# First block of a three-stage float32 kernel on unsplit weights, with a shorter float64 decoding and re-strided regrouping transfers

## The chip, the cores and the metric

The kernel runs on 1 core of one Trainium2 chip. The metric is device time in microseconds (us) of one execution, as the median of several. TensorE (PE) multiplies, VectorE (DVE) and ScalarE (ACT) do elementwise work, SyncE (SP) issues all DMAs from one queue in order.

## The reference, cut to what matters

```python
# 1. gated linear attention, 4 batches x 8 heads x 768 steps x 48 dims (float32)
new_re = ar * S_re - ai * S_im ; new_im = ar * S_im + ai * S_re
S_re, S_im = new_re + outer(k_t, v_t), new_im
y_t = q_t @ S_re
# x = y as 3072 tokens x 384
# 2. first MLP
h = x @ w_in                      # 384 -> 2048
g = h * clip(h + 3, 0, 6) / 6
x2 = g @ w_out                    # 2048 -> 384
# 3. second MLP
out = ((x2 @ w1) * (x2 @ w2) @ w3) @ w_out2
```

The weights of stages 2 and 3 arrive as float64, because they are drawn times a float64 scalar; everything else is float32.

## The kernel before, in words

**Attention.** The 24 units of 128 tokens ("chunks", six per batch) are taken in 12 groups of two. `group` (L502) computes a group's decays, phases, scaled k and q on ACT and DVE with 768-wide operations, ends with the products Kc and cs (L568, L576), and regroups them head by head with `regroup` (L570): six DMAs of 16 partitions each into KT and six into QT. `chunk` (L602) then runs a chunk on PE: transposes of Kc (L618), scores (L627) whose masked copies P are made on DVE (L630), P times v and state times q (L639, L644), and the update of the state (L653), which DVE scales by a factor that travels in two extra columns of QT (L577, L656). All these matmuls are float32: the trace shows two instructions, here called passes, for each of them.

**Splitting.** The MLP matmuls run in a faster reduced type (fp32r in the profile). So that nothing is lost, every operand is split into a high part (ACT copy) and a low part (DVE subtraction), and `mm3` (L664) multiplies three times: high x high, high x low, low x high.

**Decoding.** `load64` (L669) brings in a piece of float64 weights, `to32` (L676) turns it into float32 by integer operations on the two 32-bit words of each number: two DVE operations, three ACT operations (a scaled copy, Abs, Sign) and a DVE product. `decode` (L704) follows with `split`. The first MLP has 8 + 8 pieces of 128x768, the second 12 such pieces and 16 of 128x512.

**Blocks.** The first MLP goes in blocks of 2, 2, 4, 4, 4, 4, 4 chunks. Blocks 0 and 1 (256 tokens each) run together, block 1 seven steps behind, while the weights are still being decoded; from block 2 on a block has 512 tokens, so its matmuls are 512 columns wide. `s1` (L765) makes one of the 16 slices of h: 9 matmuls, the gate (ACT Relu, DVE product, L789 to L790), and the split of its result into gh and gl. `s2` (L796) adds the slice into three accumulators m with 9 matmuls. The copy of a group's attention output into the block's input goes by six DMAs (L586), followed by a split into xh and xl (L599, L600).

**Order.** Nothing is written out by hand. Every operation is given to `Plan.add` with an estimated duration, due times follow from pins on the MLP's matmuls, and `Plan.run` (L104) emits the instructions of each engine in the order of a simulated run. Each engine then works its list strictly in order. An edit of a duration, a dependence or a buffer can thus move instructions everywhere.

```python
def to32(raw, words, n, dst, ov):
    DVE(..., tensor_scalar(words(0) >> 29 ^ 0x40000000), [], [raw])
    DVE(..., scalar_tensor_tensor(words(1) << 3 ^ words(0)), [], [raw])
    ACT(..., words(1) <- Copy(words(1) as f32, scale=16400.0) as int), [raw], [raw])
    ACT(..., words(0) <- Abs(words(0)), [raw], [raw])
    ACT(..., words(1) <- Sign(words(1)), [raw], [raw])
    DVE(..., ov <- words(0) * words(1), [raw], [dst])
```

Of the kernel before, what the change touches and what calls it, by code (L numbers as in the profile page):

```python
# [243 lines left out]
def c_tt(n):  # L244
    return n / 960.0 + 0.07


def c_ts(n):
    return n / 1920.0 + 0.07

# [148 lines left out]
def main_kernel(tc, q, k, v, a_re, a_im, w_in, w_out, w1, w2, w3, w_out2, consts, qT, kT, arT, aiT, vT, wiT, woT, w1T, w2T, w3T, wo2T, out, blocks=(2, 2, 4, 4, 4, 4, 4)):  # L399
# [22 lines left out]
    with tc.tile_pool(name="keep", bufs=1) as kp:  # L422
      c5_ = kp.tile([128, 2, 128], F32, name="c2")
      flag = kp.tile([1, 1], I32, name="flag")
      with ctx:
# [76 lines left out]
        def group(gi):  # L502
# [42 lines left out]
            cs = nb("cs", [128, 2, KD, TG + GT])  # L545
            ACT(cA, lambda: A(cs()[:, 0, :, :TG], th(), AF.Abs), [th], [cs])
# [9 lines left out]

            def sincos():
                A(cs()[:, 1, :, :TG], th(), AF.Sin, scale=TWOPI)
                A(cs()[:, 0, :, :TG], cs()[:, 0, :, :TG], AF.Sin, scale=-TWOPI, bias=PI / 2)
# [3 lines left out]
            KT, QT = nb("KT", [96, H, TG]), nb("QT", [96, H, TG + GT])  # L563

            def prod(o, f):
                for a in range(2):
                    TT(o()[:, a, :, :TG], cs()[:, a, :, :TG], f(), ALU.mult)
# [9 lines left out]
            DVE(0.17, lambda: dve.tensor_copy(out=cs()[:, :, :, TG:], in_=G()[:, :, 127:TG:128].unsqueeze(1).to_broadcast([128, 2, KD, GT])), [G], [cs])  # L577
            regroup(QT, cs, TG + GT)
            ys = nb("ys", [128, 4, C, 128])
            for c in range(C):  # L580
                chunk(b * CPB + c0 + c, c, Kc, KT, QT, ys)

            xf = nb("xf", [128, KD, TG])
            for i in range(KD):
                for j in range(2):
                    DMA(lambda e, i=i, j=j: e.dma_start(out=xf()[64 * j:64 * j + 64, i, :], in_=ys()[64 * j + 16 * i:64 * j + 16 * i + 16].rearrange("e p c t -> e p (c t)")),  # L586
                        [ys], [xf], 180000, part=True)
            u = b * CPB + c0
            j = next(j for j, (a, n) in enumerate(blk) if a <= u < a + n)
            if j not in xbuf:  # L590
# [11 lines left out]
        def chunk(u, c_, Kc, KT, QT, ys):  # L602
# [8 lines left out]
            if not last:  # L611
                Ks = nb("Ks", [128, H, 96])
                for a in range(2):
# [6 lines left out]
                    ACT(c_act(384, True), lambda a=a, pk=pk: A(Ks()[:, :, 48 * a:48 * a + 48].rearrange("p h (t d) -> p h t d", t=KD), pk().rearrange("p (t d h) -> p h t d", t=KD, h=H), AF.Copy), [pk], [Ks], part=True)  # L620
# [27 lines left out]
            if not last:  # L648
# [7 lines left out]
                mb = lambda: QT()[:, :, TG + c_:TG + c_ + 1].to_broadcast([96, H, D])  # L656
                o_ = An.ap[:, :, 0:D]
                if first:
                    DVE(c_tt(384), lambda: TT(o_, pu(), mb(), ALU.mult), [pu, QT], [An])
                else:  # L660
                    DVE(c_tt(384), lambda: TT(o_, pu(), Ap.ap[:, :, 0:D], ALU.add), [pu, Ap], [An])
                    DVE(c_tt(384), lambda: TT(o_, o_, mb(), ALU.mult), [QT], [An])
# [13 lines left out]
        def to32(raw, words, n, dst, ov):  # L676


            DVE(c_ts(n), lambda: dve.tensor_scalar(out=words(0), in0=words(0), scalar1=29, scalar2=0x40000000, op0=ALU.logical_shift_right, op1=ALU.bitwise_xor), [], [raw])
            DVE(c_tt(n), lambda: dve.scalar_tensor_tensor(out=words(0), in0=words(1), scalar=3, in1=words(0), op0=ALU.logical_shift_left, op1=ALU.bitwise_xor), [], [raw])  # L680

            ACT(c_act(n), lambda: A(words(1), words(1).bitcast(F32), AF.Copy, scale=16400.0), [raw], [raw])
            ACT(c_act(n), lambda: A(words(0).bitcast(F32), words(0).bitcast(F32), AF.Abs), [raw], [raw])
# [20 lines left out]
        def decode(src, i, after=()):  # L704
            loads[0] += 1
            if loads[0] > EARLY:
                after = list(after) + [ready0]
# [406 lines left out]
```

## Time and profile before

| what | value |
|---|---|
| median of 3 runs | 988.65 us (987.92 to 990.36) |
| the profiled execution's own time | 994.61 us |
| its span, first to last instruction | 992.4 us |
| PE busy | 905.8 us, 91% |
| DVE busy | 602.4 us, 61% |
| ACT busy | 558.7 us, 56% |
| mean granted TensorE clock | 0.983 of full speed |
| DMA queue q1 | 101.94 MB, 40.6% of 16 engines |

PE is busy nine tenths of the span, but the share differs by stage: the page's 40 slices show PE at 0, 4, 4, 7 tenths in the first four (25 us each) and at 9 in nearly all that follow, while DVE stands at 9 and ACT at 9 to 7 in the second to the sixth. A busy PE is not a PE at its full pace: its clock has two levels, 1.2 and 2.4 GHz, and at the lower one the same instructions keep it busy twice as long.

### The profile page before, as it was taken

How to read it: one execution, taken by the hardware profiler on the slowest of the kernel's cores; microseconds unless marked ns; L12 is line 12 of the kernel's file. 1: busy time of each engine (PE TensorE's matmuls, PEld its weight loads, DVE VectorE, ACT ScalarE, POOL GpSimd, SP SyncE). 2: the span in 40 equal slices, each digit the busy share in tenths (PEclk: the TensorE clock that was granted, in tenths of full speed). 3: DMA queues.
4: the chain of work that ended last, by engine and by line, in shares of the span. 5: the costliest groups of instructions: out<-in, count | busy, mean ns of one | idle time of the engine just before them, and what ended most of it. 6: DMA issues, size and time to landing. Idle time of an engine off the chain costs nothing.

```text
span 992.4 us, 13406 instructions
## 1 busy us (share of the span) xinstructions
PE 905.8 (91%) x5178; PEld 781.8 (79%) x5178; DVE 602.4 (61%) x931; ACT 558.7 (56%) x895; POOL 0.2 (0%) x4
## 2 busy tenths in 40 slices
PE   0447999889999999899999999999999999999996
PEld 0437989768887888788788878789888888888886
DVE  6899999888498839784854546995232323222221
ACT  7999998778387648565742455894121212121211
POOL 0000000000000000000000000000000000000000
PEclk9999999879999999799999999999999999999999
DMA  6896147772786086507632544732010100000000
GB/s 248 170 378 125 30 96 148 147 125 59 108 207 165 27 150 149 165 22 132 152 99 42 116 152 159 296 118 86 1 51 13 50 14 24 20 10 24 5 28 35
DMA packets 56375, 102.87 MB, mean 104 GB/s; under 512 B 6768, under 2 KB 34544, under 8 KB 56304
## 3 DMA queue, kind: packets, MB, share of 16 engines
q1 hardware_dynamic: 56304, 101.94, 40.6%
q8 instruction: 42, 0.69, 0.3%
q14 instruction: 29, 0.24, 0.1%
HBM read 64.62 MB, written 13.63 MB: 79 GB/s over the span
## 4 chain that ended last, share of the span: by engine, by line
PE 69%; ACT 15%; DVE 7%; DMA 4%; SPq 2%; issue 2%; ACTq 0%; DVEq 0%
PE x L666 12%; PE x L667 12%; PE x L665 12%; PE m L665 5%; ACT W L483 5%; PE m L666 4%; PE m L667 4%; ACT u L483 3%; PE x L627 3%; PE m L996 3%; PE m L994 3%; PE m L995 3%; ACT L1032 2%; PE x L639 1%; PE x L653 1%
## 5 line engine op out<-in xcount | busy, mean ns | idle before, releaser
L483 ACT ACTIVATE r<-x 128x512 f32<-128x512 f32 (+1 forms) x160 | 88.2, 551 | 155.2 <-PE x L667 129.4
L486 DVE TENSOR_TENSOR r<-r,x 128x512 f32<-128x512 f32 x48 | 33.0, 688 | 179.4 <-PE x L667 179.4
L665 PE MATMUL m<-gh,W 128*128 128x512 f32 (+1 forms) x336 | 126.8, 377 | 1.4 <-ACT gh L483 1.3
L666 PE MATMUL m<-gl,W 128*128 128x512 f32 (+1 forms) x336 | 124.2, 370 | 2.3 <-DVE gl L486 2.2
L483 ACT ACTIVATE W<-W 128x768 f32<-128x768 int32 (+6 forms) x153 | 121.0, 834 | 8.3 <-DVE W L680 7.1
L667 PE MATMUL m<-gh,W 128*128 128x512 f32 (+1 forms) x336 | 123.3, 367 | 0.1
L665 PE MATMUL x<-xh,W 128*128 128x512 f32 (+1 forms) x288 | 113.4, 394 | 3.8 <-ACT xh L483 3.8
L486 DVE TENSOR_TENSOR gl<-r,gh 128x512 fp32r<-128x512 f32 (+1 forms) x112 | 68.3, 611 | 78.6 <-ACT gh L483 78.3
L666 PE MATMUL x<-xl,W 128*128 128x512 f32 (+1 forms) x288 | 111.6, 387 | 3.2 <-DVE xl L486 3.2
L667 PE MATMUL x<-xh,W 128*128 128x512 f32 (+1 forms) x288 | 110.6, 384 | 0.0
L483 ACT ACTIVATE gh<-r 128x512 fp32r<-128x512 f32 (+1 forms) x112 | 63.7, 569 | 78.1 <-PE m L667 73.6
L666 PE MATMUL x<-W 128*128 128x512 f32 (+1 forms) x228 | 84.2, 369 | 0.0
L667 PE MATMUL x<-W 128*128 128x512 f32 (+1 forms) x228 | 84.2, 369 | 0.0
L665 PE MATMUL x<-W 128*128 128x512 f32 (+1 forms) x228 | 83.9, 368 | 0.0
L790 DVE SCALAR_TENSOR_TENSOR r<-r,x 128x512 f32<-128x512 f32 (+1 forms) x112 | 67.9, 606 | 25.4 <-ACT r L483 24.5
L666 PEld LDWEIGHTS m<-gl,W 128*128 128x128 f32 x336 | 64.3, 192 | 15.1 <-DVE gl L486 4.9
L665 PEld LDWEIGHTS m<-gh,W 128*128 128x128 f32 x336 | 64.3, 191 | 14.6 <-issue 2.4
L667 PEld LDWEIGHTS m<-gh,W 128*128 128x128 f32 x336 | 64.2, 191 | 11.2 <-DVE W L486 0.3
L665 PEld LDWEIGHTS x<-xh,W 128*128 128x128 f32 x288 | 56.2, 195 | 15.4 <-ACT xh L483 4.8
L666 PEld LDWEIGHTS x<-xl,W 128*128 128x128 f32 x288 | 56.3, 195 | 14.7 <-DVE xl L486 4.4
L667 PEld LDWEIGHTS x<-xh,W 128*128 128x128 f32 x288 | 56.2, 195 | 11.2
L627 PE MATMUL x<-QT,KT 96*128 96x128 f32 x384 | 54.2, 300 | 8.8 <-issue 3.3
(194 smaller groups left out, 1810.7 us busy)
## 6 DMA issues: line engine op xcount, KB each, us to landing
QT<-cs SPq DMA_DIRECT2D x72, 129.0 KB, 6.5
KT<-Kc SPq DMA_DIRECT2D x72, 128.0 KB, 5.3
W<-in_w3T_dram SPq DMA_DIRECT2D x16, 512.0 KB, 4.8
v<-in_vT_dram SPq DMA_DIRECT2D x24, 256.0 KB, 5.0
W<-in_wiT_dram SPq DMA_DIRECT2D x8, 768.0 KB, 11.7
W<-in_woT_dram SPq DMA_DIRECT2D x8, 768.0 KB, 13.1
ar<-in_arT_dram SPq DMA_DIRECT2D x12, 384.0 KB, 3.6
ai<-in_aiT_dram SPq DMA_DIRECT2D x12, 384.0 KB, 3.2
```

The costliest lines, as they stand in the source:

```text
L483: act.activation(out=o, in_=i, func=f, scale=scale, bias=bias, **kw)
L486: dve.tensor_tensor(out=o, in0=i0, in1=i1, op=op)
L627: pe.matmul(p_()[:, i, :], KT()[:, 4 * g + i, tok], QT()[:, 4 * g + i, tok])
L639: pe.matmul(py()[64 * j:64 * j + 64, p, :], vb.ap[:, h, :], Pm[h // 4]()[:, h % 4, :], start=True, stop=first, tile_position=(0, 64 * j), ...
L665: pe.matmul(o, wh, xh, start=start, stop=False, **kw)
L666: pe.matmul(o, wh, xl, start=False, stop=False, **kw)
L667: pe.matmul(o, wl, xh, start=False, stop=stop, **kw)
L790: DVE(c_tt(n), lambda: dve.scalar_tensor_tensor(out=r()[:, :n], in0=r()[:, :n], scalar=6.0, in1=h()[:, :n], op0=ALU.min, op1=ALU.mult), [h ...
L994: pe.matmul(o, gh()[:, a], Wb()[:, 0, i % 2], start=(i == 0), stop=False)
L995: pe.matmul(o, gh()[:, a], Wb()[:, 1, i % 2], start=False, stop=False)
L996: pe.matmul(o, gl()[:, a], Wb()[:, 0, i % 2], start=False, stop=(i == KI - 1))
L1032: P.run(lambda t_: act.preload_act_table_set(t_), window=48, hold=2.24)
```

## The change

- **Block 0 unsplit** (`NATIVE = 1`). The input of block 0 is written by the transfers straight into the tile xh and read as float32; there is no split of it. Its `s1` and `s2` take one float32 matmul where three fp32r ones stood, on the decoded but unsplit weights. The gate writes its tile (gh or gl, by turns) and is not split.
- **Splits follow.** `decode` no longer ends with `split`; the 16 splits of the first MLP's weights are now asked for by block 1.
- **Decoding.** `to32` has one ACT operation (a copy scaled by 2^-112) and a last DVE operation that puts sign and magnitude together; Abs and Sign are gone.
- **Regrouping.** A head's 48 rows are now ordered d*3+t where they were t*16+d, so each regrouping DMA goes to 16 partitions with a step of 3 where it went to 16 neighbours. The state's factor gets a tile of its own, mt, filled by six small DMAs per group. The planner is told smaller sizes for these transfers (800*w where it was 1408*w, 100000 where it was 180000).
- **Paced loads.** A load of first-MLP weights from the sixth on waits until the piece five before it has been taken up by DVE (`AHEAD`).

```diff
-                        DMA(lambda e, a=a, t=t: e.dma_start(out=dst()[48 * a + 16 * t:48 * a + 16 * t + 16], in_=src()[:, a, t, :]),
-                            [src], [dst], 1408 * w, part=True)
+                        DMA(lambda e, a=a, t=t: e.dma_start(out=dst()[48 * a + t:48 * a + 48:KD], in_=src()[:, a, t, :]),
+                            [src], [dst], 800 * w, part=True)
...
+            DVE(0.17, lambda: dve.tensor_copy(out=ge(), in_=G()[:, :, 127:TG:128]), [G], [ge])
+            for a in range(2):
+                for t in range(KD):
+                    DMA(lambda e, a=a, t=t: e.dma_start(out=mt()[48 * a + t:48 * a + 48:KD], in_=ge()[:, t, :]), [ge], [mt], 60000, part=True)
...
-            DVE(0.17, lambda: dve.tensor_copy(out=cs()[:, :, :, TG:], in_=G()[:, :, 127:TG:128]...), [G], [cs])
...
+            if j < NATIVE:
+                xf = SB("xh", [128, KD, NMAX], 1, F32R)
+                xbuf[j] = (xf, xf, xf, xf)
...
+            if j < NATIVE:
+                return
...
+            ACT(c_act(n), lambda: A(words(1).bitcast(F32), words(1).bitcast(F32), AF.Copy, scale=2.0 ** -112), [raw], [hi_])
+            DVE(c_ts(n), lambda: dve.tensor_scalar(out=words(0), in0=words(0), scalar1=29, ..., op0=ALU.logical_shift_right), [raw], [lo_])
+            DVE(c_tt(n), lambda: dve.scalar_tensor_tensor(out=words(0), in0=words(1), scalar=3, in1=words(0), op0=ALU.logical_shift_left, op1=ALU.bitwise_or), [hi_], [lo_])
+            DVE(c_tt(n), lambda: dve.scalar_tensor_tensor(out=ov().bitcast(I32), in0=words(1), scalar=-0x80000000, in1=words(0), op0=ALU.bitwise_and, op1=ALU.bitwise_or), [lo_], [dst])
+            return lo_
...
+        EARLY, AHEAD = 4, 5
+        taken_up = []
         def decode(src, i, after=()):
+            n_ = len(taken_up)
+            after = list(after) + ([ready0] if n_ >= EARLY else []) + ([taken_up[n_ - AHEAD]] if n_ >= AHEAD else [])
...
-            to32(raw, words, 768, raw, f)
-            return split(raw, f), shape
+            taken_up.append(to32(raw, words, 768, raw, f))
+            return raw, shape
...
+            if j == NATIVE and f % 2 == 0:
+                for w_ in (wi, wo):
+                    raw, shape = w_[f // 2]
+                    w_[f // 2] = split(raw, packed(raw, 768)), shape
...
+                    if whole:
+                        wf = packed(w, 768)().rearrange("p (a b) -> p a b", a=shape[0])
+                        pe.matmul(h()[:, :n], wf[:, kk, o:o + 128], xh()[:, kk, :n].bitcast(F32), start=kk == 0, stop=kk == KD - 1)
...
+            if whole:
+                gh = SB(("gh", "gl")[f % 2], ...)
+                ACT(..., lambda: A(gf(), h()[:, :n], AF.Relu, bias=3.0), [h], [gh], boost=MB)
+                DVE(..., scalar_tensor_tensor(out=gf(), in0=gf(), scalar=6.0, in1=h()[:, :n], op0=ALU.min, op1=ALU.mult), [h], [gh], boost=MB)
+                return gh, gh
```

In `s2` the same replacement stands with gh read as float32. New line numbers: the decoding's DVE operations are L696, L697 and L698, block 0's matmuls L806 and L837, its gate L815, the attention's transposes, scores, P times v, state times q and update L634, L643, L655, L660 and L669, `mm3` L681 to L683.

On PE, before, where block 0's first matmuls come (v and Ks are a chunk's values and keys, c the identity, W weights, xh and xl the split input):

```order
L653 MATMUL x<-v_71,Ks 96x48 x8
L618 MATMUL x<-c_58,Kc 128x128 x6
L665 MATMUL x<-xh,W 128x256
L666 MATMUL x<-xl,W 128x256
L667 MATMUL x<-xh,W 128x256
```

The same place now, from the last attention matmul of chunk 1 on (m are the accumulators of block 0):

```order
L660 MATMUL x<-QT,A_73 64x128 x2
L806 MATMUL x<-xh,W 128x256 x9
L634 MATMUL x<-c_58,Kc 128x128 x6
L837 MATMUL m_481<-gh,W 128x256
L837 MATMUL m_483<-gh,W 128x256
L837 MATMUL m_485<-gh,W 128x256
L669 MATMUL x<-v_71,Ks 96x48 x8
```

Three slices of h now stand ahead of chunk 2's transposes and update, which stood ahead of block 0.

Further on in PE's new list, where chunk 2's scores and its P times v stand between block 0's matmuls:

```order
L643 MATMUL x<-QT,KT 128x128 x8
L806 MATMUL x<-xh,W 128x256 x3
L837 MATMUL m_481<-gh,W 128x256
L837 MATMUL m_483<-gh,W 128x256
L837 MATMUL m_485<-gh,W 128x256
L655 MATMUL x<-P_574,v_71 64x128 x2
L660 MATMUL x<-QT,A_74 64x128 x2
```

All of it is float32; the first fp32r matmul of the whole list (L681, block 1) now stands behind 78 of block 0's 96 matmuls.

On DVE, before, from the low part of block 0's input to the first low part of a gate's result (r is the gate's tile, s a tile of group 2):

```order
L486 TENSOR_TENSOR xl<-xf,xh 128x3x256
L486 TENSOR_TENSOR W<-W 128x768 x3
L680 SCALAR_TENSOR_TENSOR W<-W 128x768
L790 SCALAR_TENSOR_TENSOR r<-r,x 128x256
L486 TENSOR_TENSOR W<-W 128x768
L486 TENSOR_TENSOR s_333<-s_333,u 128x768
L486 TENSOR_TENSOR gl<-r,gh 128x256
```

The place of the first gates now:

```order
L490 TENSOR_TENSOR Kc<-cs,k 128x768 x2
L815 SCALAR_TENSOR_TENSOR gh<-gh,x 128x256
L490 TENSOR_TENSOR cs<-cs,q 128x768 x2
L815 SCALAR_TENSOR_TENSOR gl<-gl,x 128x256
L697 SCALAR_TENSOR_TENSOR W<-W 128x768
```

The gates now come between the products of group 1, ahead of most of the decoding, and nothing follows a gate before PE may use it.

## Rows read from the trace of the kernel before

**Rows 1.** Busy time by stage: us, PE, PEld, DVE, ACT, POOL (instructions), PEclk, DMA share, GB/s.
```profile
0.00:81.90 81.90, 27.90 (x152) 23.74 (x152) 68.88 (x104) 73.03 (x97) 0.20 (x4) 1.00 0.84 263
...
125.00:183.00 58.00, 53.79 (x480) 51.70 (x478) 56.02 (x101) 51.18 (x95) 0.00 (x0) 1.00 0.68 127
...
206.00:420.00 214.00, 208.20 (x1193) 172.51 (x1193) 161.20 (x245) 143.14 (x224) 0.00 (x0) 0.96 0.58 128
420.00:700.00 280.00, 274.20 (x1513) 229.54 (x1512) 178.74 (x271) 164.63 (x268) 0.00 (x0) 1.00 0.45 122
```

**Rows 2.** Timeline: start us, us, engine, line, operation [idle before <- releaser].
```profile
59.22 0.68 DVE L486 TENSOR_TENSOR P<-x,c 128x512 f32<-128x512 f32 x1
...
63.91 8.86 SPq L586 DMA_DIRECT2D xf<-ys  x6
...
81.02 0.86 ACT L483 ACTIVATE xh<-xf 128x768 fp32r<-128x768 f32 x1
...
81.93 0.58 PE L665 MATMUL x<-xh,W 128*128 128x256 f32 x1 [1.63 <-ACT xh L483]
...
205.89 0.77 PE L665 MATMUL x<-xh,W 128*128 128x512 f32 x1
```

**Rows 3.** Groups by line and shape: busy us, mean ns of one, idle before it.
```profile
L680 DVE SCALAR_TENSOR_TENSOR W<-W 128x768 int32<-128x768 int32 x28 | 26.6, 952 | 0.0
...
L483 ACT ACTIVATE W<-W 128x768 f32<-128x768 int32 x28 | 26.0, 927 | 0.0
L483 ACT ACTIVATE W<-W 128x768 f32<-128x768 f32 x28 | 25.8, 926 | 0.0
...
L486 DVE TENSOR_TENSOR gl<-r,gh 128x256 fp32r<-128x256 f32 x32 | 13.3, 418 | 0.5 <-ACT gh L483 0.2
L483 ACT ACTIVATE gh<-r 128x256 fp32r<-128x256 f32 x32 | 13.3, 416 | 0.3 <-PE m L667 0.3
...
L483 ACT ACTIVATE xh<-xf 128x768 fp32r<-128x768 f32 x11 | 9.3, 845 | 6.4 <-DMA xf<-ys 4.5 <-PE x L667 1.9
```

**Rows 4.** Pieces of the chain that ended last: start us, us, what.
```profile
164.40 1.79 PE x L627 x16
...
233.03 0.81 PE x L618 x6
...
463.20 1.32 PE x L653 x16
464.51 1.02 PE x L639 x16
```

**Rows 5.** Timeline of PE in the early stage, columns as in rows 2.
```profile
46.39 3.75 PE L627 MATMUL x<-QT,KT 96*128 96x128 f32 x16 [3.33 <-issue]
...
58.49 0.70 PE L639 MATMUL x<-P,v 128*64 128x128 f32 x4 [0.45 <-DVE P L486]
...
61.53 0.64 PE L644 MATMUL x<-QT,A 96*64 96x128 f32 x4
```

**Rows 6.** Timeline of PE, fp32r matmuls of 256 columns, two stretches.
```profile
84.59 0.41 PE L667 MATMUL x<-xh,W 128*128 128x256 f32 x1
...
85.87 0.41 PE L667 MATMUL x<-xh,W 128*128 128x256 f32 x1
...
87.90 0.28 PE L665 MATMUL x<-xh,W 128*128 128x256 f32 x1
...
88.49 0.28 PE L667 MATMUL x<-xh,W 128*128 128x256 f32 x1
```

**Rows 7.** PE by stretch: us, PE busy (instructions), PEclk, DMA share, GB/s.
```profile
183.40:186.70 3.30, 3.30 (x17) 0.50 0.24 57
186.80:190.10 3.30, 3.30 (x20) 0.50 0.26 74
190.20:195.70 5.50, 5.50 (x72) 1.00 0.63 212
```

**Rows 8.** DMA issues by line: KB each, median us to landing.
```profile
KT<-Kc SPq DMA_DIRECT2D x72, 128.0 KB, 5.3
```

More of the change, by code (lines that the diff above doesn't have):

```diff
@@ L544, in group @@
                 A_prev["ce"] = ce
-            cs = nb("cs", [128, 2, KD, TG + GT])
-            ACT(cA, lambda: A(cs()[:, 0, :, :TG], th(), AF.Abs), [th], [cs])
+            cs = nb("cs", [128, 2, KD, TG])
+            ACT(cA, lambda: A(cs()[:, 0], th(), AF.Abs), [th], [cs])
+            mt = nb("mt", [96, H, GT], 2)
+            ge = nb("ge", [128, KD, GT], 2)
             y, sq = nb("u"), nb("u")
@@ L699, in pieces @@
             return src[i].rearrange("p (a b) -> p a b", a=a), (a, 768 // a)
-        EARLY = 4
-        loads = [0]
+        EARLY, AHEAD = 4, 5
+        taken_up = []
         def decode(src, i, after=()):
-            loads[0] += 1
-            if loads[0] > EARLY:
-                after = list(after) + [ready0]
+            n_ = len(taken_up)
+            after = list(after) + ([ready0] if n_ >= EARLY else []) + ([taken_up[n_ - AHEAD]] if n_ >= AHEAD else [])
             src, shape = pieces(src, i)
@@ L798, in s2 @@
             w, shape = wo[f // 2]
-            wh, wl = lambda: part(w, 0, shape), lambda: part(w, 1, shape)
             gh, gl = g
+            whole = j < NATIVE
             def mm():
+                kw = {"skip_group_check": True} if j < 2 else {}
                 for m in range(KD):
                     a = slice(m * 128, m * 128 + 128)
-                    mm3(acc[m]()[:, at:at + n], wh()[:, f % 2, a], wl()[:, f % 2, a], gh()[:, :n], gl()[:, :n], f == 0 and at == 0, f == KF - 1, **({"skip_group_check": True} if j < 2 else {}))
+                    if whole:
+                        wf = packed(w, 768)().rearrange("p (a b) -> p a b", a=shape[0])
+                        pe.matmul(acc[m]()[:, at:at + n], wf[:, f % 2, a], gh()[:, :n].bitcast(F32), start=f == 0 and at == 0, stop=f == KF - 1, **kw)
+                    else:
+                        wh, wl = part(w, 0, shape), part(w, 1, shape)
+                        mm3(acc[m]()[:, at:at + n], wh[:, f % 2, a], wl[:, f % 2, a], gh()[:, :n], gl()[:, :n], f == 0 and at == 0, f == KF - 1, **kw)
             for x in acc:
                 x.part = True
-            PE(9 * c_mm(n), mm, [w, gh, gl] + ([opened] if at else []), acc + [own] + ([] if at or f else [opened]), pin=pins["2", j, f])
+            PE(3 * c_m4(n) if whole else 9 * c_mm(n), mm, [w, gh, gl] + ([opened] if at else []), acc + [own] + ([] if at or f else [opened]), pin=pins["2", j, f])
         gens = [group(g) for g in range(NG)]
@@ L896, in later @@
             if tags is None:
-                return decode(src, g, after)
+                raw, shape = decode(src, g, after)
+                return split(raw, packed(raw, 768)), shape
             src, shape = pieces(src, g)
```

61 lines of the change are left out of this document (33 added, 28 removed).

## The prediction

> **What bounds the kernel now.** I read the stages first [rows 1]. After 206 us PE is busy for 208.2 of 214 us and 274.2 of 280 us: there the time is PE's work, and whatever ACT or DVE is spared moves the end only through the 11.6 us in which PE still waits. Up to 81.9 us it is the other way: PE is busy 27.9 us, ACT 73.0 and DVE 68.9 of 81.9. From 125 to 183 us both kinds are nearly full (PE 53.8, DVE 56.0 of 58 us). So the change can earn something only before about 206 us, where block 2 starts its 512-wide matmuls [rows 2]. I use that start as the mark: what it gains, the end gains, less the work that is pushed behind it.
>
> The timeline shows how block 0 gets started [rows 2]: the last mask of chunk 1 at 59.2, six transfers of its output issued over 8.9 us from 63.9 on, the ACT split only at 81.0, the first matmul at 81.9. PE has nothing but scraps of attention until then.
>
> **The change, part by part.**
>
> *Decoding.* Two ACT operations of 926 and 927 ns go per 128x768 piece [rows 3]; the last DVE operation keeps its length if it costs what the like integer operation costs, 952 ns. For 16 pieces this frees 16 x 1.85 = 29.7 us of ACT before block 2. ACT's copies of gh, 16 x 0.416 = 6.7 us, and of xh, 0.85 us, go too; DVE loses only 16 x 0.418 = 6.7 us of gl and about 0.95 us of xl. DVE was as full as ACT, so ACT's 37 us are mostly cover: they don't shorten the stage by themselves, DVE's 8 us might.
>
> *Start of block 0.* By the order, DVE has, ahead of the last mask of chunk 1, one shift (0.55 us) and three operations of group 1 (0.95 us each) fewer: some 3.1 us, so transfers start at 63.9 - 3.1 = 60.8. Before, they took 8.9 us to issue behind eleven weight loads; now loads are paced and I take 3.5 us for the issues and 3.3 us for landing, like the shorter of these transfers elsewhere: 60.8 + 6.8 = **67.6 us** for the first matmul, against 81.9. The bounds are 65 (DVE waits a little less for ACT) and 73 (issue as slow as before).
>
> *Block 0's matmuls.* Float32 scores run 16 passes of 128 columns in 1.79 us [rows 4] when the clock is at 2.4 GHz, so a pass of 256 columns costs 0.224 us; at 1.2 GHz 3.75 us [rows 5], 0.47 us, or twice the 0.213 us of an fp32r matmul at that level [rows 6], 0.43. I take 0.45. Block 0 has 96 matmuls, 192 passes: 43.0 us at the upper level, where 288 fp32r matmuls at 0.118 us [rows 6] cost 34.0. That is +9.0 us of PE work, beside work only as long as PE would idle anyway.
>
> *The clock* is the open question. An fp32r stretch brought it up: 0.213 us per matmul until 85.9, 0.118 from 87.9 on [rows 6]. An unbroken float32 stretch did not: from 183.4 to 186.7 PE was busy all the time with scores, at a granted 0.50, and stayed there until nine fp32r matmuls and state updates had run; from 190.2 it had 1.00 [rows 7]. So I expect block 0's first matmuls to run at 1.2 GHz, and take the dense P times v of chunk 2, two narrow passes side by side, as what brings the clock up. The trace has no such stretch inside dense work: the only one at 1.2 GHz, 58.5 to 62.2 [rows 5], has idle time on both sides. Hence this is the widest bound. The Trainium skill's page "TensorE: Matmul & The Clock Gate", section "What's actually happening", says that the default state is throttled and activity releases it, with no exception for float32. By that the clock would rise with block 0's first matmuls; the stretch at 183.4 us speaks against it, and the sum below does not use it (rival 2 does).
>
> *The sum up to the mark,* by PE's list. At 1.2 GHz from 67.6: 60 passes of block 0, 27.0; transposes 2 x 0.81 = 1.6, update 2 x 1.32 = 2.6 [rows 4], scores 3.75, P times v and state times q 3.7 [rows 5]; 38.7 in all, to 106.3. Then at 2.4 GHz: 96 passes 21.5, scores 1.8, P times v 2.0, transposes 0.8, update 1.3: 27.4, to 133.7. Then the mixed list up to the mark: 261 fp32r matmuls 30.8; 36 passes of block 0, 8.1; four groups of scores 7.2; 112 narrow passes at 1.02 / 16 = 0.064, 7.2; transposes 2.4; updates 2.6: 58.3, to 192.0. In the like stretch before, 125 to 183 us, PE was idle 4.2 of 58; I add 4. The mark comes at **196**, 9.9 us earlier than 205.9.
>
> *What is pushed behind the mark.* By the order, 16 state-update matmuls (2 x 1.32), six transposes (0.8) and 27 fp32r matmuls (27 x 0.118 = 3.2) stood ahead of it and now follow: +6.6 us.
>
> *After the mark.* ACT is relieved of 12 x 1.85 and, at about 0.67 us for 512 wide, of 16 x 1.34, in all 43.7 us. PE's waits there are 11.6 us, and a clock of 0.96 over 214 us means 17 us at the lower level, or 8.6 us lost [rows 1]. I take 4 us of these 20 as recovered, bounds 0 and 15.
>
> *Small parts.* The ge copies replace the old copies of the factor one for one: nothing. The mt transfers put 72 more issues of about 0.6 us on SP, 3.5 us a group; a group has some 33 us of SP time before 420 us: cover, unless they delay the issue of a later load. The stepped regrouping can take time off KT's 5.3 us [rows 8]; PE waits for it once early, 3.3 us at 46.4 [rows 5], but DVE's list, not the scores, sets the last mask, so the sum takes nothing. If transfers to stepped partitions were slower, the same wait would grow and the mark would slip by as much.
>
> Sum: -9.9 + 6.6 - 4 = -7.3 us. The profiled execution took 994.6 us, some 6 us more than the median; I apply the difference to the median: 988.65 - 7.3 = **981.3 us**.
>
> **The rivals.**
>
> 1. *The clock stays down through block 0 (slower).* Place: the 156 passes of block 0 ahead of the first fp32r matmul. At 1.2 GHz all the way: 70.2 us, with twice the attention's 11.8 us (23.6), from 67.6 to 161.4; then 58.3 and about 3 us until the clock is up: mark at 222.7. That is +16.8 + 6.6 - 4 = +19.4: **1008 us**. For it: the float32 stretch at 183.4 [rows 7]. Against: narrow passes side by side were never tried dense. It decides from here: every microsecond longer at the lower level after 106 costs half a microsecond, so the 7.3 us are gone if the clock is not up by about 121 us, the end of chunk 3's P times v.
>
> 2. *The clock rises at once (much faster).* As at 81.9, some 5.7 us after the first matmul, at 73.3: 33 us of work at the lower level become 16.5, the mark comes at 179.5, and the sum is -26.4 + 6.6 - 4 = -24: **965 us**. DVE could follow: it loses little work, but it is full, so not much below. Against: rows 7.
>
> 3. *No change.* The clock comes up only with chunk 3, or falls again while DVE's in-order list makes PE wait for gates; or the transfers stay slow and block 0 starts at 73. The mark then comes at 201 to 206 and its gain is eaten by the 6.6 us: **988 us**. That the transfers' new step does nothing at all belongs here and costs my sum nothing, since no term rests on it.
>
> **How the numbers follow.** Forecast 0.42, rival 1 0.27, rival 2 0.18, rival 3 0.13. About 0.3% (3 us) is what a measurement of this kernel can tell from no change. The forecast's own spread (mark 190 to 200, recovery 0 to 15) is 972 to 987, nearly all faster; rival 3 lies mostly within 0.3%. Faster: 0.40 + 0.18 = 0.58; same 0.14; slower 0.28. The range for 8 in 10 reaches from 961, a little past rival 2, to 1004, into rival 1 with a somewhat earlier start. The likeliest case alone spans 972 to 987.
>
> **What would show it.** The first block-0 matmul at 65 to 70 us; passes of 256 columns some 0.43 to 0.47 us apart at first and 0.22 after chunk 2's P times v, near 106; ACT well below DVE between 50 and 175 us; the first 512-wide matmul at 190 to 200. If passes are still 0.43 apart at 125, rival 1 has it; if they are 0.22 apart at 75, rival 2. If the mark comes early and the time doesn't fall, the step on the work behind the mark is wrong, and PE's waits after it must have grown.

## The result and the profile after

The change takes 957.49 us in the median of 4 runs (954.36 to 963.3), against 988.92 us of the kernel before in the same session: ratio 0.9688, 95% interval 0.9634 to 0.9742, 31 us faster. The prediction said 981.3 us, 961 to 1004: the sign was right, the size was not, and the time lies 3.5 us below the range. The profiled execution is the slowest of the four, 963.3 us with a span of 961.1 us, and the one before was slow for its kernel too (994.6 us), so I compare spans: 992.4 before, 961.1 after, 31.3 us less.

The engines' busy time on the page of the change (PE had 905.8 us before):

```profile
PE 898.6 (93%) x5082; PEld 772.0 (80%) x5082; DVE 592.7 (62%) x914; ACT 495.1 (52%) x790; POOL 0.2 (0%) x4
```

The stages of the change, columns as in [rows 1]:

```profile
0.00:62.80 62.80, 21.11 (x124) 18.57 (x124) 51.90 (x81) 54.20 (x72) 0.20 (x4) 0.97 0.69 238
62.80:125.00 62.20, 59.26 (x371) 52.59 (x372) 58.54 (x87) 42.84 (x69) 0.00 (x0) 0.92 0.51 141
125.00:183.00 58.00, 52.23 (x434) 48.56 (x433) 48.48 (x84) 39.25 (x71) 0.00 (x0) 0.94 0.51 142
185.00:400.00 215.00, 213.18 (x1276) 175.99 (x1276) 182.29 (x278) 160.00 (x251) 0.00 (x0) 1.00 0.50 136
400.00:680.00 280.00, 277.49 (x1549) 233.83 (x1548) 176.55 (x269) 133.22 (x219) 0.00 (x0) 1.00 0.41 124
```

From 185 us on PE is idle 1.8 + 2.5 = 4.3 us where it was idle 5.8 + 5.8 = 11.6 us [rows 1], and its clock is not down in these two stretches; before it stood at 0.96 over 214 us. Before the mark, DVE is no longer full from 125 us on, and ACT has a third of its time free.

The start of block 0 and the mark, as in [rows 2]:

```profile
58.01 3.81 SPq L602 DMA_DIRECT2D xh<-ys  x6
...
62.84 5.53 PE L806 MATMUL x<-xh,W 128*128 128x256 f32 x18 [6.67 <-DMA xh<-ys]
...
68.20 1.07 PE L634 MATMUL x<-c,Kc 128*128 128x128 f32 x6
...
184.84 0.48 PE L681 MATMUL x<-xh,W 128*128 128x512 f32 x1
```

The first matmul of block 0 is 19.1 us earlier than before, the first 512-wide matmul (the mark) 21.1 us earlier: 184.8 against 205.9. The clock in the first five microseconds of block 0, columns as in [rows 1]:

```profile
62.90:65.50 2.60, 2.60 (x6) 2.09 (x7) 2.60 (x5) 2.59 (x4) 0.00 (x0) 0.50 0.68 197
65.60:68.10 2.50, 2.50 (x13) 2.21 (x12) 2.50 (x5) 2.13 (x6) 0.00 (x0) 0.98 0.72 257
```

Six passes took 2.60 us, 0.43 each, then thirteen took 2.50 us: the clock went from 1.2 to 2.4 GHz at 65.7 us, after 2.9 us of float32 work.

The rest of the gain stands behind the mark: 992.4 - 205.9 = 786.5 us before, 961.1 - 184.8 = 776.3 us now. PE in the two stretches, columns as in [rows 7], before and now:

```profile
205.90:992.40 786.50, 767.04 (x4076) 0.99 0.34 87
184.80:961.10 776.30, 764.16 (x4142) 1.00 0.31 91
```

That is 10.2 us less, although the order pushed 6.6 us of PE work there (66 instructions more), so 16.8 us were recovered. PE's longest waits of that stretch, before (206 to 700 us), columns us in total, times, longest:

```profile
PE x L627 <- ACT Ks L483: 2.6, 1, 2.6
PE x L665 <- ACT xh L483: 2.2, 2, 1.5
PE x L666 <- DVE xl L486: 2.2, 3, 1.0
PE m L946 <- ACT x2s L483: 1.4, 1, 1.4
PE x L653 <- ACT Ks L483: 1.3, 2, 0.7
```

and with the change (185 to 680 us):

```profile
PE m L681 <- ACT gh L487: 1.8, 2, 1.0
PE m L682 <- DVE gl L490: 1.1, 3, 0.6
PE x L643 <- DMA v<-in_vT_dram: 1.1, 1, 1.1
```

The waits behind Ks, xh and xl are gone. Transfers land sooner: KT took 5.3 us in [rows 8], QT 6.5 us on the page of the kernel before, and q1's share was 40.6%. Now:

```profile
q1 hardware_dynamic: 66672, 101.95, 35.9%
...
KT<-Kc SPq DMA_DIRECT2D x72, 128.0 KB, 3.5
QT<-cs SPq DMA_DIRECT2D x72, 128.0 KB, 3.6
```

So the questions for the chip were: which part brings the gain, why did the clock rise so early, and why did so much come back behind the mark.

### The profile page after: what moved, and what is told of

It reads as the page before. It is cut to its first block, busy times and chain, and to the rows that moved or that the text cites. A ratio compares the mean times of both kernels' runs of the same rounds, so it can differ in the third digit from the quotient of the medians.

```text
span 961.1 us, 13166 instructions
## 1 busy us (share of the span) xinstructions
PE 898.6 (93%) x5082; PEld 772.0 (80%) x5082; DVE 592.7 (62%) x914; ACT 495.1 (52%) x790; POOL 0.2 (0%) x4
## 4 chain that ended last, share of the span: by engine, by line
PE 63%; DVE 14%; DMA 8%; ACT 7%; SPq 4%; issue 2%; DVEq 0%; ACTq 0%
PE x L681 10%; PE x L682 10%; PE x L683 10%; PE m L682 4%; PE m L683 4%; PE m L681 4%; PE m L1032 3%; PE m L1030 3%; PE m L1031 3%; SPq L584 3%; PE x L643 2%; ACT u L487 2%; DMA W<-in_w3T_dram 2%; DMA QT<-cs 2%; ACT L1068 1%
## 5 line engine op out<-in xcount | busy, mean ns | idle before, releaser
L681 PE MATMUL m<-gh,W 128*128 128x512 f32 (+1 forms) x288 | 110.9, 385 | 1.9 <-ACT gh L487 1.8
L682 PE MATMUL m<-gl,W 128*128 128x512 f32 (+1 forms) x288 | 109.5, 380 | 1.4 <-DVE gl L490 1.1
L683 PE MATMUL m<-gh,W 128*128 128x512 f32 (+1 forms) x288 | 108.7, 378 | 0.0
L681 PE MATMUL x<-xh,W 128*128 128x512 f32 x240 | 97.5, 406 | 0.1
L682 PE MATMUL x<-xl,W 128*128 128x512 f32 x240 | 95.0, 396 | 0.1
L683 PE MATMUL x<-xh,W 128*128 128x512 f32 x240 | 94.9, 396 | 0.0
L681 PE MATMUL x<-W 128*128 128x512 f32 (+1 forms) x228 | 84.7, 371 | 0.1
L683 PE MATMUL x<-W 128*128 128x512 f32 (+1 forms) x228 | 84.0, 369 | 0.0
L487 ACT ACTIVATE W<-W 128x768 f32<-128x768 f32 (+2 forms) x65 | 53.4, 833 | 27.7 <-DMA W<-in_w3T_dram 8.0
L682 PEld LDWEIGHTS m<-gl,W 128*128 128x128 f32 x288 | 54.6, 190 | 14.3 <-DVE gl L490 4.1
L681 PEld LDWEIGHTS m<-gh,W 128*128 128x128 f32 x288 | 54.6, 190 | 13.2 <-ACT gh L487 2.7
L683 PEld LDWEIGHTS m<-gh,W 128*128 128x128 f32 x288 | 54.6, 189 | 10.4
L643 PE MATMUL x<-QT,KT 96*128 96x128 f32 x384 | 53.9, 298 | 6.4 <-DMA QT<-cs 5.0
L643 PEld LDWEIGHTS x<-QT,KT 96*128 96x128 f32 x384 | 51.6, 212 | 9.0 <-issue 4.0
L487 ACT ACTIVATE u<-r 128x512 fp32r<-128x512 f32 x36 | 22.8, 633 | 63.7 <-DVE r L490 63.7
L681 PEld LDWEIGHTS x<-xh,W 128*128 128x128 f32 x240 | 45.1, 188 | 10.9 <-issue 1.0
```

The source lines that it names most:

```text
L487: act.activation(out=o, in_=i, func=f, scale=scale, bias=bias, **kw)
L643: pe.matmul(p_()[:, i, :], KT()[:, 4 * g + i, tok], QT()[:, 4 * g + i, tok])
L681: pe.matmul(o, wh, xh, start=start, stop=False, **kw)
L682: pe.matmul(o, wh, xl, start=False, stop=False, **kw)
L683: pe.matmul(o, wl, xh, start=False, stop=stop, **kw)
```

## The experiments

Times are medians, ratios are to the kernel before in the same session, with 95% intervals. Runs named a_ start from the change, runs named b_ from the kernel before. "Mark" is the first 512-wide matmul of the profiled execution, "low" how long the granted clock stood at 1.2 GHz behind it, the last 5 to 9 us of the kernel apart. The kernel before read 988.9 to 991.3 us in these sessions, so across sessions the ratios compare better than the times.

| run | us | ratio | mark | low |
|---|---|---|---|---|
| before | 988.9 | 1 | 205.9 | 18 |
| the change | 957.5 | 0.9688 (0.9634 to 0.9742) | 184.8 | 0 |
| a_split0 | 975.9 | 0.9876 (0.9845 to 0.9908) | 198.5 | 6 |
| a_olddec | 973.7 | 0.9832 (0.9811 to 0.9852) | 194.6 | 5 |
| a_oldreg | 994.8 | 1.0062 (1.0040 to 1.0083) | 193.5 | 20 |
| a_nopace | 976.2 | 0.9875 (0.9855 to 0.9894) | 192.8 | 7 |
| b_newreg | 987.3 | 0.9977 (0.9960 to 0.9995) | 201.9 | 16 |
| b_newdec | 968.8 | 0.9787 (0.9769 to 0.9805) | 196.7 | 3 |
| a_native_only | 1023.0 | 1.0338 (1.0310 to 1.0367) | 208.9 | 27 |
| b_dec_order | 990.5 | 1.0004 (0.9985 to 1.0022) | 201.7 | 19 |
| b_dec_reg | 969.8 | 0.9799 (0.9770 to 0.9828) | 196.0 | 3 |
| a_mtq | 962.8 | 0.9741 (0.9701 to 0.9782) | 192.4 | 1 |
| a_ahead6 | 963.3 | 0.9722 (0.9691 to 0.9754) | 191.2 | 3 |
| b_dec_burden | 1017.8 | 1.0292 (1.0251 to 1.0332) | 217.7 | 33 |
| a_burden | 1005.9 | 1.0175 (1.0135 to 1.0216) | 198.5 | 27 |
| a_oldreg_sizes | 971.6 | 0.9817 (0.9777 to 0.9857) | 190.7 | 10 |
| b_native | 981.4 | 0.9915 (0.9886 to 0.9943) | 195.0 | 10 |
| a_sizes1000 | 953.7 | 0.9637 (0.9617 to 0.9656) | 180.2 | 0 |
| a_sizes1200 | 959.5 | 0.9703 (0.9687 to 0.9720) | 188.2 | 0 |

### Undoing one part of the change

The theories were A, float32 block 0; B, the lighter decoding; C, the faster regrouping.

```diff
-        NATIVE = 1
+        NATIVE = 0
```

> The change with one thing undone: block 0 of the first projection runs on split weights again (fp32r matmuls), everything else stays. Theory A, float32 block 0 is what brings the gain before the mark (no split in the way, an early start, a clock that is up): the first 512-wide matmul goes back from 184.8 us to 196 or later and the time rises from 957.5 by 10 to 20 us, to 967 to 977. Theory B, the lighter decoding, and theory C, the faster regrouping, bring it: the splits cost DVE some 8 us and ACT some 7 us, but block 0 costs PE 9 us less, so the mark stays within 5 us of 184.8 and the time within 5 us of 957.5. In both, the clock is up within some 6 us of block 0's first matmul.

Block 0 on split weights took 975.9 us, with the mark at 198.5: these are theory A's numbers. But block 0 started at 63.7 us here too, so the early start is not float32's doing. What came back is waits, the longest on either side of the mark (columns as above), with a lower clock from 191 to 205 us:

```profile
PE x L634 <- DVE Kc L490: 5.1, 1, 5.1
PE x L681 <- ACT xh L487: 4.5, 1, 4.5
```

```diff
-            ACT(..., A(words(1).bitcast(F32), ..., AF.Copy, scale=2.0 ** -112), [raw], [hi_])
+            ACT(..., A(words(1), words(1).bitcast(F32), AF.Copy, scale=16400.0), [raw], [raw])
+            ACT(..., A(words(0)..., AF.Abs), [raw], [raw])
+            ACT(..., A(words(1)..., AF.Sign), [raw], [raw])
```

> The change with the old decoding (three ACT operations and three DVE operations for each piece, as before the change), everything else stays. Theory B, ACT's relief is what brings the gain: ACT is near full again from 50 to 125 us, the mark comes at 195 or later, PE's idle gaps after the mark grow from 4.7 us to 10 or more with the clock falling in them, and the time is 967 to 980. Theory A (float32 block 0) and theory C (regrouping): ACT has room for it; mark within 4 us, time 957 to 962.

Undoing the decoding costs 16 us, with the mark at 194.6: this is theory B's time as well, though PE's waits behind the mark grew only from 5.4 to 9.2 us.

```diff
-out=dst()[48 * a + t:48 * a + 48:KD]
+out=dst()[48 * a + 16 * t:48 * a + 16 * t + 16]
```

(the same for mt and for block inputs, with the host's row order to match; every engine's list of instructions stays the change's, word for word)

> The change with the regrouping transfers of keys, gates and block-0 input put back to 16 neighbouring partitions each (same number of issues, same order of the work), everything else stays. Theory C, the stepped partitions bring part of the gain: KT takes 5.3 us again to land instead of 3.5, block 0's first matmul starts 2 to 5 us later than 62.8, PE's gaps grow, and the time is 962 to 968. Theories A and B: landing times hide behind other work and the time stays at 956 to 961.

It cost 37 us, five times what theory C expected. PE's waits for transfers in this run, over the whole span:

```profile
PE x L643 <- DMA mt<-ge: 12.0, 3, 5.4
PE x L643 <- DMA QT<-cs: 8.7, 3, 6.1
```

QT takes 6.0 us to land instead of 3.6, KT 4.5 instead of 3.5, and block 0 still starts at 63.0 us. Of the 31.2 us longer span, PE's idle time is 82.6 - 62.5 = 20.1 and PE's busy time 909.7 - 898.6 = 11.1: seven of its idle stretches were followed by some 3 to 7 us at 1.2 GHz.

```diff
-        EARLY, AHEAD = 4, 5
+        EARLY, AHEAD = 4, 100
```

> The change without the pacing of the weight loads (they are issued as early as their buffers allow), everything else stays. If pacing is what frees the queue for block 0's transfers, their issue is again stuck behind weight loads: first matmul of block 0 at 66 to 72 us instead of 62.8, time 960 to 968. If the early transfers only wait for DVE, nothing moves: 955 to 960.

The first matmul of block 0 came at 68.2, and xh took 7.4 us to landing instead of 3.3. That is as expected, but the time rose by 19 us, more than the expected 3 to 11 and than the 5.4 us of that delay. Theories A and B thus had their numbers, and C five times its own. None can be the reason by itself: the four undone parts cost 18 + 16 + 37 + 19 = 90 us, and the whole change brings 31. Only a_oldreg kept the change's order; for the other three the planner made a new one.

### Doing one part alone

```diff
-out=dst()[48 * a + 16 * t:48 * a + 16 * t + 16]
+out=dst()[48 * a + t:48 * a + 48:KD]
```

> The kernel before with one part of the change: the regrouping transfers go to 16 partitions with a step of 3 (same issues, same planner sizes, same order of the work). Theory C, the step alone brings much of the gain: KT and QT land in 3.5 to 4 us instead of 5.3 and 6.5, PE's waits of over 0.3 us after the first 512-wide matmul fall from 12.7 to 6 or less, the stretches at the lower clock there (24 us but for the last ones) mostly go, and the time falls from 989 to 970 to 982. Rival: landing times lie beside other work as long as block 0 is split and ACT is full: 985 to 990.

KT and QT land in 4.1 us instead of 5.3 and 6.5, in an unchanged order, and the time falls by 2 us: the rival's number, theory C falls for the kernel before.

```diff
-            ACT(..., AF.Copy, scale=16400.0) ; ACT(..., AF.Abs) ; ACT(..., AF.Sign)
+            ACT(..., AF.Copy, scale=2.0 ** -112)
```

(with the DVE operations of the change's `to32`)

> The kernel before with one part of the change: the decoding with one ACT operation. If ACT's relief pays by itself (51 us less of ACT in all): first 512-wide matmul at 200 or earlier, time 970 to 980. If DVE, just as full, keeps the pace: ACT's busy time falls by 51 us, the mark moves by less than 3 us, and the time is 983 to 990.

This took 968.8 us, two thirds of the gain, a little below the first case's 970, with the mark at 196.7. ACT's busy time fell from 558.7 to 501.2. Behind the mark, PE's stretch is 17.1 us shorter than before with nearly the same instructions (columns as in [rows 7]):

```profile
196.74:966.10 769.36, 757.76 (x4070) 0.99 0.36 89
```

But the planner is told of cheaper operations, and it wrote other lists for all engines.

```diff
-        EARLY, AHEAD = 4, 5
+        EARLY, AHEAD = 4, 100
-out=dst()[48 * a + t:48 * a + 48:KD]
+out=dst()[48 * a + 16 * t:48 * a + 16 * t + 16]
-            ACT(..., AF.Copy, scale=2.0 ** -112)
+            ACT(..., AF.Copy, scale=16400.0) ; ACT(..., AF.Abs) ; ACT(..., AF.Sign)
```

> The change with the decoding, the neighbouring partitions and the unpaced loads of before; what is left of it is block 0 on unsplit float32 weights, with splits that follow it, and the tile for the state's factor. If the parts add up, undoing these three from 957.5 costs 16 + 37 + 19 us: about 1030. If they overlap (each takes away the same waits), it is 990 to 1005; if float32 block 0 pays by itself, it is 972 to 985.

This took 1023.0 us, slower than before by 33 and near the 1030 of adding up: undone together, the three cost 65 of the 72 us that they cost one by one. What the change brings does not add up in this way. The planner is still told of the short transfers here, as in a_oldreg.

```diff
+        NATIVE = 1
-            return split(raw, f), shape
+            return raw, shape
```

(in the kernel before, with the code for an unsplit block and the later splits)

> The kernel before with float32 block 0 alone: old decoding, neighbouring partitions, planner sizes of before, unpaced loads, and the factor still in QT. If float32 block 0 by itself is what made the run with the three other parts undone slow (1023): 1005 to 1025. If it was the factor's own 72 transfers to neighbouring partitions that did: 980 to 992. If float32 block 0 pays in any setting: 965 to 980.

This took 981.4 us, the middle case's number: float32 block 0 by itself, in an order made for it, pays 8 us, and it isn't what made a_native_only slow. That run differs from this one by the factor's own transfers and by a planner told of `800 * w` for transfers that are no shorter; these two weren't told apart.

### Load or order

```diff
+            DVE(c_ts(n), ... words(0) >> 29 ..., [], [raw])
+            DVE(c_tt(n), lambda: None, [], [raw])
+            ACT(c_act(n), ... words(1) * 2.0 ** -112 ..., [raw], [raw])
+            ACT(c_act(n), lambda: None, [raw], [raw])
+            ACT(c_act(n), lambda: None, [raw], [raw])
+            DVE(c_tt(n), join, [raw], [dst])   # the two DVE operations that follow
```

> The kernel before with the decoding of one ACT operation, but with the planner told of the old operations, so that the order of the instructions of every engine stays that of before, but for the decoding's own. It tells whether the lighter decoding pays by ACT's time (the 20 us that the decoding alone brought come for the most part here too: 968 to 975, PE's waits behind ACT after the first 512-wide matmul mostly gone) or by the other order that the planner made with it (983 to 990, waits as before).

ACT is busy 502.4 us, as light as in b_newdec, every list is that of before but for the decoding's own operations, and nothing is gained: 990.5 us, ratio 1.0004. One place shows why, in this run's timelines of PE and of ACT (columns as in [rows 2]):

```profile
399.14 0.82 PE L618 MATMUL x<-c,Kc 128*128 128x128 f32 x6
404.61 1.80 PE L627 MATMUL x<-QT,KT 96*128 96x128 f32 x8 [4.66 <-ACT Ks L483]
```

```profile
400.76 0.84 ACT L483 ACTIVATE u<-s 128x768 f32<-128x768 f32 x1 [3.60 <-DVE s L486]
401.64 0.84 ACT L483 ACTIVATE u<-u 128x768 f32<-128x768 f32 x1
...
403.35 0.83 ACT L483 ACTIVATE cs<-ai 128x768 f32<-128x768 f32 x1
404.09 0.47 ACT L483 ACTIVATE Ks<-x 128x384 f32<-128x384 f32 x1
```

The transposes are done by 400 us. ACT has time, it even waits 3.6 us for DVE, but its list has a group's operations ahead of the Ks copy, and PE stands until 404.6 us; from 404.9 to 415.2 us its clock is at 1.2 GHz. The same place of the kernel before:

```profile
408.03 1.57 PE L627 MATMUL x<-QT,KT 96*128 96x128 f32 x8 [2.63 <-ACT Ks L483]
```

So the list kept a wait there, 2.6 us before and 4.7 now, and ACT's freed time did not shorten it. This run also moves one DVE operation of each decoding to the place of the next; what that costs was not measured apart. At the like place of b_newdec, whose list has other work between the two:

```profile
400.28 0.82 PE L618 MATMUL x<-c,Kc 128*128 128x128 f32 x6
...
403.04 1.48 PE L653 MATMUL x<-v,Ks 128*96 128x48 f32 x16
```

No wait stands there. The other corner of the square puts ACT's load back into the new order:

```diff
             A(words(1)..., AF.Copy, scale=2.0 ** -112)
+            A(words(1)..., words(1)..., AF.Copy)
+            A(words(1)..., words(1)..., AF.Copy)
```

> The kernel before with the new decoding, in the order the planner makes for it (968.8 us), but with two copies in place added behind each of ACT's decoding copies, so that ACT has its old load again in the new order. With the run that had the old order and the light load (990.5) it makes the square of order and load. If only the order counts: 966 to 972. If the new order needs the light load: 980 to 1000, with PE's waits behind ACT back after the first 512-wide matmul.

This took 1017.8 us, 49 more than without the copies. ACT is busy 570.4 us, 11.7 more than before, which alone is far from 49. The waits after the mark (218 to 740 us) are back behind ACT and what follows it:

```profile
PE x L653 <- ACT Ks L483: 5.8, 2, 3.7
PE m L665 <- ACT gh L483: 5.5, 4, 3.7
PE m L666 <- DVE gl L486: 4.4, 6, 2.1
```

> The change in its own order, with the same two copies added behind each of ACT's decoding copies. If ACT's relief counts in this order: 970 to 990 (undoing the decoding with a new order cost 16 us). If it is covered here too: 956 to 963.

The change's own order with the same burden took 1005.9 us, 48 more, with ACT busy 563.4 us. In the table, the old load is that of the kernel before in the first row and the two added copies in the others:

| | old load of ACT | light load |
|---|---|---|
| order of before | 988.9 | 990.5 |
| order made for the new decoding | 1017.8 | 968.8 |
| order of the change | 1005.9 | 957.5 |

The light load alone is worth nothing, the new order alone costs 29 us, both together bring 20. The order spends the time that the decoding frees. The 20 us are also more than the 6 to 8 us by which small edits of the order move the time (below).

The same square for the transfers: with the light step in the order of before, 2 us; the old step in the change's order, 37 us lost; and the old step in an order made for it:

```diff
-                            [src], [dst], 800 * w, part=True)
+                            [src], [dst], 1408 * w, part=True)
-                        [ys], [xf], 100000, part=True)
+                        [ys], [xf], 180000, part=True)
```

(on top of a_oldreg)

> The change with neighbouring partitions, as in the run that cost 37 us, but with the planner told the transfer sizes of before (1408*w, 180000), so that it makes an order for longer transfers. If the 37 us came from an order drawn up for short transfers: 965 to 980. If slow transfers cost it in any order, with the factor's 72 more transfers in the queue: 985 to 1000.

This took 971.6 us. Told the old transfer sizes, the planner wins back 23 of the 37 us: PE has no wait for mt or QT among its seven longest any more, though QT still takes 6.0 us to land. With an order made for each, the regrouping is then worth 14 us in the change.

```diff
-out=dst()[48 * a + 16 * t:48 * a + 16 * t + 16]
+out=dst()[48 * a + t:48 * a + 48:KD]
```

(on top of b_newdec, whose lists it keeps word for word)

> The kernel before with the new decoding and the stepped regrouping, in the order of the run with the new decoding alone (block 0 split, factor in QT, loads not paced). If the step pays once ACT is out of the way: 955 to 964, as fast as the whole change, and then float32 block 0 and the pacing bring nothing. If it brings as little as it did alone (2 us): 965 to 969, and the rest of the change has to account for the last 8 to 11 us.

It took 969.8 against 968.8 us: the step brings nothing here either. The last 11 us need the rest of the change.

### How much is the luck of an order

```diff
-            regroup(QT, cs, TG)
+            DVE(0.17, ... cs()[:, :, :, TG:] <- factor ..., [G], [cs])
+            regroup(QT, cs, TG + GT)
-                mb = lambda: mt()[:, :, c_:c_ + 1].to_broadcast([96, H, D])
+                mb = lambda: QT()[:, :, TG + c_:TG + c_ + 1].to_broadcast([96, H, D])
```

> The change with the state's factor back in two extra columns of QT: 72 small transfers fewer, the rest as in the change. If these transfers hold up the queue (3.8 us of it per group), QT lands earlier and the time falls to 948 to 956. If they cost nothing, 955 to 962; if they pay, because the factor comes before QT and the update need not wait for the last of QT, it is 965 to 980.

This took 962.8 us, between the cases; its interval overlaps the change's, so it isn't settled whether the factor's own transfers cost anything.

```diff
-        EARLY, AHEAD = 4, 5
+        EARLY, AHEAD = 4, 6
```

> The change with loads paced six pieces back where they are paced five back: hardly another load schedule, but the planner makes another order of it. It shows how much of the differences between these kernels is the luck of an order: 955 to 961 if a part is worth what undoing it cost, 965 to 975 if the order of the change is a lucky one and any other loses some ten microseconds.

This took 963.3 us, between the cases. By its ratio it is 3 us above the change, and the intervals overlap, so this run alone does not settle what another order costs; the next two do.

```diff
-                            [src], [dst], 800 * w, part=True)
+                            [src], [dst], 1000 * w, part=True)
```

> The change with the planner told 1000*w for the transfers to KT and QT where it is told 800*w, so that its order allows for a landing about 1 us later; it still shows PE waits for QT of 2.7 and 2.3 us. If the order is what counts, such waits go: 948 to 956. Within the spread that another order makes (the two runs with small edits stood at 963): 957 to 965.

This took 953.7 us, the fastest here, at a ratio of 0.9637 (0.9617 to 0.9656); the intervals of this run and of the change overlap. The largest wait for QT is 1.3 us where two of 2.7 and 2.3 were, and between the end of its start-up, at 65 us, and its last 8 us the clock is never down.

> The same with 1200*w, an order that allows for a landing about 2 us later: 948 to 956 if waits for QT go and nothing else is late for it, 957 to 970 if the order is only another one.

(The same line with `1200 * w`.) This took 959.5 us, so the order is only another one: a 3.4 us wait for Kc stands at 180 us instead. The two differ by 5.8 us, and a_sizes1000 and a_ahead6 by 8 in their ratios, each time with the intervals apart. Differences of 6 to 8 us between these kernels can thus come from the order alone and say nothing of the part.

### What brings the clock up

> A kernel that computes nothing of the reference (it writes zeros) and runs seven stretches of unbroken matmuls on PE, with some ten microseconds without PE work between them: float32 scores' shape (96 rows, 128 columns, 32 matmuls), float32 128 rows and 128 columns (32), 96 rows and 256 columns (16), block 0's shape 128 rows and 256 columns (16), two narrow passes side by side (64), fp32r 128 rows and 256 columns (32), and the first again. Theory A, any unbroken float32 work brings the clock up if it lasts: in every stretch the matmuls go from the slow price (0.47 us for the scores' two passes, 0.9 for 256 columns) to half of it within some 3 to 7 us. Theory B, the shape decides: the stretches of 96 rows and 128 columns stay at 0.47 us for all of their 15 us, the one of 128 rows and 256 columns rises within 3 us as in block 0, and the others tell whether rows or columns matter.

The timeline of PE in that kernel (sA to sG are the operands of the seven stretches, in the order of the text above):

```profile
36.13 9.18 PE L48 MATMUL p<-sB 128*128 128x128 f32 x64 [11.80 <-ACT sB L35]
57.10 10.45 PE L48 MATMUL p<-sC 96*128 96x256 f32 x32 [11.79 <-ACT sC L35]
79.34 9.58 PE L48 MATMUL p<-sD 128*128 128x256 f32 x32 [11.79 <-ACT sD L35]
100.71 9.14 PE L53 MATMUL p<-sE 128*64 128x128 f32 x128 [11.79 <-ACT sE L35]
121.66 5.64 PE L48 MATMUL p<-sF 128*128 128x256 f32 x32 [11.81 <-ACT sF L35]
139.10 10.54 PE L48 MATMUL p<-sG 96*128 96x128 f32 x64 [11.79 <-ACT sG L35]
```

and two of its stretches cut where the clock rose, columns as in [rows 1]: 128 rows by 256 columns (block 0's shape), then the scores' shape.

```profile
79.40:84.20 4.80, 4.80 (x12) 3.82 (x13) 0.00 (x0) 0.76 (x1) 0.00 (x0) 0.50 0.00 0
84.20:88.90 4.70, 4.70 (x22) 3.83 (x20) 0.00 (x0) 0.00 (x0) 0.00 (x0) 1.00 0.00 0
...
139.10:145.70 6.60, 6.60 (x31) 6.60 (x32) 0.00 (x0) 0.82 (x1) 0.00 (x0) 0.50 0.00 0
145.70:149.60 3.90, 3.90 (x35) 3.74 (x34) 0.00 (x0) 0.00 (x0) 0.00 (x0) 1.00 0.00 0
```

Theory A holds: every shape brought the clock up, float32 scores of 96 rows by 128 columns included. The six rises came 3.8, 6.7, 4.9, 4.0, 3.5 and 6.6 us after the stretch began. They follow no order of rows, columns or type: 96 rows by 256 columns took 6.7, two narrow passes side by side 4.0, fp32r 3.5. The first stretch, of the same shape as the last, went to half the price after 4.7 us where the last took 6.6, so the shape alone does not set the time (its lines stand in the last section).

## Why the prediction was wrong, point by point

**Where two steps failed.** The sum was -9.9 + 6.6 - 4 = -7.3. Measured: -21.1 before the mark, and 10.2 us less behind it, that is +6.6 and -16.8 if the pushed work is taken as I counted it. Eleven microseconds are missing ahead of the mark and thirteen behind it. The eleven ahead are three terms of the sum. Block 0 started 4.8 us earlier than 67.6. The lower clock was put at 38.7 us and measured at 16.5 from that start to the mark, which at half pace is worth 11.1 us. PE idled 8.7 us there where 4 were allowed, 4.7 us more. Together -4.8 - 11.1 + 4.7 = -11.2. The thirteen behind are the term "4 us recovered", which measured 16.8.

**The clock.** "So I expect block 0's first matmuls to run at 1.2 GHz", up to 106 us: wrong. It rose at 65.7. I had read "An unbroken float32 stretch did not" bring it up from [rows 7]; the run on the clock shows that very shape rising 6.6 us into its stretch. The rows showed 3.3 us of scores and then nine fp32r matmuls and updates until 190.2, and I put down to the type what was only time. The Trainium skill's page "TensorE: Matmul & The Clock Gate", section "What's actually happening", that activity releases a throttled default with no exception for float32, was right: this trace and the clock run agree, with 2.9 and with 3.5 to 6.7 us. Rival 2's mechanism was the true one. Its mark of 179.5 was 5.3 us too early in spite of the earlier start, because the clock fell again at 79.3 to 86.2, 130.5 to 134.0 and 168.1 to 171.5 us, after waits for QT, QT and ys; at half pace these 13.7 us cost 6.8, and because of the 8.7 us of idle time.

**The first matmul.** 62.84 us, below my bounds of 65 to 73. The transfers were issued from 58.0, not 60.8; and I added 3.5 us of issue and 3.3 us of landing, where the matmul started 4.8 us after the first issue: landing lies beside issuing.

**Block 0's price.** 0.43 us a pass at 1.2 GHz, and six passes in 1.29 us, 0.215 each, at 98.5 us with the clock up: as estimated (0.45 and 0.224).

**After the mark.** "I take 4 us of these 20 as recovered, bounds 0 and 15": measured 16.8. PE's idle time fell from 11.6 to 4.3 us, and the 18 us at the lower clock, worth 9, went with it. The two go together: the clock had been at the lower level behind such waits, at 408.6 us for one. The decoding in an order made for it is enough for this: b_newdec alone has 17.1 us less behind its mark, and b_dec_order, with the same decoding in the order of before, has none (786.6 beside 786.5 us). It is not the only way: a_olddec, with the old decoding, still has 7.5 us less (973.6 - 194.6 = 779.0).

**Decoding.** "ACT's 37 us are mostly cover": that held literally in the order of before (b_dec_order, 0 us), and yet it is the step that failed most, since the 4 us behind the mark rest on it. I costed the freed time against a fixed list. The list is not fixed: the planner takes the new durations and makes an order that the old load couldn't have kept (b_dec_burden, +49 us). The decoding with its order brings 20 us by itself, of the 31.

**Regrouping.** "the sum takes nothing": right for the step alone (2 us), wrong for the change, whose order relies on it: undoing it costs 14 us with an order made anew, 37 without. The 3.3 us at 46.4 that I put down to KT have "issue" as their releaser in [rows 5], so that row does not show a wait for it.

**Pacing.** The issue came free as I said; undoing the pacing cost 19 us, with the spread of 6 to 8 us that another order has.

**The range.** Rival 2 at 965 was the nearest case, with 0.18. No rival combined a clock that rises at once with most of the 20 us behind the mark; -26.4 + 6.6 - 16.8 would have been 952.

What stays open: which places of the new lists carry the 20 us one by one (one of them, at 404.6 us, is shown), and how much of the last 11 us is float32 block 0: it is worth 8 us by itself and 18 where it was undone, with a re-made order both times, and 6 to 8 us can be the order's luck.

## What to carry to other kernels

Where a planner orders the instructions, cost an edit twice: in the old order, where freed time behind an in-order list is cover, and in the order that the planner will make, which spends what it is told. The converse is the danger: an order made for durations that the chip doesn't keep cost 37 to 49 us here, more than the whole change brings. Undoing a part while the order is kept prices the order's reliance on it and not the part: of the transfers' 37 us, 14 were left with an order made anew. And parts undone one by one need not add up to the gain: with orders made anew they cost 18 + 16 + 14 + 19 = 67 us, and the gain is 31.

## What the runs showed of the hardware

- The same clock rose 2.9 us into block 0, 4.7 and 6.6 us into two stretches of scores of the clock kernel and 6.9 us into the mixed work at 183.3 us of the kernel before: 3.3 us of one shape at 1.2 GHz are no sign of what the shape does.
- The transfers of 128 KB to 16 partitions each, six to a tile, land in 4.1 us (median) with a step of 3 and in 5.3 (KT) and 6.5 us (QT) to neighbours, with all lists the same (b_newreg); the queue's share of the 16 engines' time fell from 40.6 to 35.2% for the same bytes. The Trainium skill's page "SBUF — State Buffer", section "Door 1: The DMA port swizzle (why `[64,N]` ≈ `[32,N]`)", gives a map from partitions to ports by which, as an estimate, 16 neighbours lie on 4 ports and 16 with a step of 3 on 8 or more; the direction agrees, no run counted ports.
- The granted clock reads 1.00 in these traces until the first change on record, even where the price says 1.2 GHz. In the clock kernel's first stretch, columns as in [rows 1]:

```profile
14.70:19.30 4.60, 4.60 (x21) 4.60 (x22) 0.00 (x0) 0.82 (x1) 0.00 (x0) 1.00 0.24 89
19.40:24.30 4.90, 4.90 (x44) 4.74 (x43) 0.00 (x0) 0.00 (x0) 0.00 (x0) 1.00 0.00 0
```

There were 21 passes in 4.6 us, then 44 in 4.9, at the same reading. Early stretches are to be read by the price of a known matmul. In the kernel before the reading is 1.00 in the first stage of [rows 1] and at 84.6 to 85.9 us, where the fp32r matmuls of [rows 6] have the slow price, so its mean of 0.983 leaves its slow start out.
